# Ones woven between pairs of x tiles for a 65-column read matmul, and x transposed by DMA block by block

## The chip, the cores and the metric

The kernel runs on one core of a Trainium2 chip. The time is device microseconds (us) of that core. The kernel before takes 156.45 us, the median of three runs (155.93 to 156.77). The profile comes from one further execution, of 155.67 us, whose recorded span is 153.8 us.

## What is computed

A cross-attention between 512 tokens and 32 state rows for each of 8 batches and 8 heads, followed by a maxout feed-forward layer on the 8 x 544 = 4352 rows that it gives:

```python
scores = scale * x @ state.T                # per batch and head: 512 x 32
xread  = softmax(scores) @ state            # 512 x 64
sread  = softmax(scale * state @ x.T) @ x   # 32 x 64
rows   = concat([xread, sread], axis=2)     # heads side by side: 544 x 512 per batch
h      = max(rows @ w1, rows @ w2, rows @ w3)   # 512 -> 768
out    = h @ w_out                              # 768 -> 512
```

Both softmaxes use the same exponentials: `exp(scores)` is normalised along the states for `xread` and along the tokens for `sread`. So `sread` is a matmul of the exponentials with x, and its denominators are the same exponentials times a column of ones.

## The kernel before

All data is cast to bf16. The tokens of a batch lie as 128 partitions by 4 (`j`), so x of one batch is one tile of 128 x 2048, with 64 columns of ones behind it (width `XW + D`, lines 66 and 437). GpSimd issues the loads, one DMA of 512 KB (as written) per batch (`load_x`, line 70). For the products x must be transposed: for batches 0 to 2 TensorE does it (`x_transpose`, line 174, with a copy out of PSUM at line 178); for batches 3 to 7 one DMA transpose of the whole tile does it, 128 x 2048 into 16 blocks of 128 x 128, issued from the SyncE queue (`x_transpose_dma`, line 182). The rest of a batch goes as follows.

- `scores` (L196) multiplies the transposed x, 16 blocks as stationary operand, with the states, and ScalarE takes the exponential into `e` (L201).
- `softmax` (L208 to L211) gives the normalised `a`; its last multiplication runs on GpSimd. `a_transpose_dma` (L227) transposes `a` into `aT`, one DMA transpose of 8 blocks, for batches 3 to 7.
- The first layer's weights are folded with the states first: `G` = state x w1, w2, w3 (L271, L278 and L281), so `x_maxout` multiplies `aT` with `G` directly (L343), and ScalarE and VectorE take the maximum of three products (L347, L350, L351). `ffn_out` is the second layer (L381, copied out at L384, stored at L392 and L395).
- `sread` (L241) does 32 matmuls a batch, with 32 columns of `e` as stationary operand and 128 moving columns: 64 columns of x and the 64 ones. Four heads' results share a PSUM tile by rows, at column tiles of the array. VectorE takes the reciprocal of the denominators and multiplies (L246, L248), giving `sr`; a small DMA transpose of one 128 x 128 block puts it into `ats` (L249). Its issue is put off in the list `late`.
- The 256 rows of `sread` of all batches go through the feed-forward layer as a batch "s", interleaved with batch 7.

The schedule is manual: each engine runs its instructions in the order in which the program writes them, and so does the SyncE queue. From batch 2 on, a loop over `b` lays the work of batch `n = b + 1` into six slots between the six `x_maxout` blocks of batch `b`: `scores(n)` in slot 0, `softmax(n)` in slot 1, `a_transpose_dma(n)` and then `x_transpose_dma(n + 2)` in slot 2, `sread(n)` in slot 4, and the put-off `ats` transposes in slot 5. So `aT` of batch n is issued after x of batch n + 1 and before x of batch n + 2, and `x_maxout(n, 0)` needs that `aT`. The tile `xT` has three buffers. On the SyncE queue the order from the first DMA transpose on is: xT of batch 3; the states of two pairs of batches (`stT`, L143); `ats` of batches 0, 1 and 2; xT 4; aT 3; xT 5; ats 3; aT 4; xT 6; ats 4; aT 5; xT 7; ats 5; aT 6; ats 6; aT 7; ats 7; and then stores.

Of the kernel before, what the change touches and what calls it, by code (L numbers as in the profile page):

```python
# [8 lines left out]
F32 = mybir.dt.float32  # L9
BF16 = mybir.dt.bfloat16  # L10
AX = mybir.AxisListType
# [4 lines left out]
def kernel(  # L16
# [14 lines left out]
    nc = tc.nc  # L31

    B, H, S, D = x.shape
# [8 lines left out]
    J = 4  # L42
    HS = H // 2
    NM = d_ff // 128
    XW = H * J * D
# [3 lines left out]
    data = ctx.enter_context(tc.tile_pool(name="data", bufs=1))  # L49
    wpool = ctx.enter_context(tc.tile_pool(name="weights", bufs=1))  # L50
    work = ctx.enter_context(tc.tile_pool(name="work", bufs=2))
    pp = ctx.enter_context(tc.tile_pool(name="pp", bufs=2, space=bass.MemoryType.PSUM))
# [10 lines left out]
    load_st(0, nc.sync)  # L63


    x_sb = [data.tile([128, XW + D], BF16, name=f"x{b}") for b in range(B)]
    xv = [t[:, 0:XW].rearrange("p (h j d) -> p h j d", j=J, d=D) for t in x_sb]

    def load_x(b):
        nc.gpsimd.dma_start(  # L70
            out=x_sb[b][:, 0:XW].rearrange("p (h jd) -> p h jd", h=H),
            in_=x[b].rearrange("h (p j) d -> p h (j d)", j=J))

    def x_heads(b, g):
        return (x_sb[b][:, 0:XW].rearrange("p (s g jd) -> g p s jd", g=2, s=HS)[g],
# [10 lines left out]
    ident = const.tile([128, 128], BF16, name="ident")  # L86
# [73 lines left out]
    xT, e, a, aT, G, ht, osb = {}, {}, {}, {}, {}, {}, {}  # L160

    def new(d, b, shape, name, bufs=2):
        d[b] = work.tile(shape, BF16, tag=name, bufs=bufs, name=name)

    def x_transpose(b, g, *copies):

        if g == 0:
            new(xT, b, [128, H, 2, 128], "xT", bufs=3)
        n = HS // len(copies)
        for k, copy in enumerate(copies):  # L170
            p = pp.tile([128, n, 2, 128], BF16, tag="pw", bufs=4, name="pxt")
            for s in range(n):
                for jj in range(2):
                    nc.tensor.transpose(  # L174
                        p[:, s, jj, :],
                        xv[b][:, 2 * (n * k + s) + g, 2 * jj:2 * jj + 2, :].rearrange("p j d -> p (j d)"),
                        ident)
            copy(out=xT[b].rearrange("p (s g) j t -> p g s j t", g=2)[:, g, n * k:n * k + n], in_=p)  # L178

    def x_transpose_dma(b):  # L180
        new(xT, b, [128, H, 2, 128], "xT", bufs=3)
        nc.sync.dma_start_transpose(out=xT[b].rearrange("p h j t -> p (h j) t"), in_=x_sb[b][:, 0:XW])

    def scores(b, g0, g1):
        n = g1 - g0
# [45 lines left out]

    def sread(b):

        p = pp.tile([128, 2, 2, D], F32, tag="pw", bufs=4, name="psr")
        for j in range(J):
            for g in range(2):
                for s in range(HS):
                    xj = xv[b][:, 2 * s + g, j, :]
                    both = bass.AP(xj.tensor, xj.offset,
                                   (xj.ap[0], (XW - ((2 * s + g) * J + j) * D, 2), (1, D)))  # L240
                    nc.tensor.matmul(  # L241
                        p[32 * s:32 * s + 32, g], e[b][:, j, g, s, :], both,
                        start=(j == 0 and g == 0), stop=(j == J - 1), skip_group_check=True,
                        tile_position=(0, 32 * s))
        rd = work.tile([128, 2, 1], F32, tag="rd", name="rd")
        nc.vector.reciprocal(out=rd, in_=p[:, :, 1, 0:1])  # L246
        sr = work.tile([128, 2, D], BF16, tag="sr", bufs=B, name="sr")
        nc.vector.tensor_mul(out=sr, in0=p[:, :, 0, :], in1=rd.to_broadcast((128, 2, D)))  # L248
        late.append(lambda: nc.sync.dma_start_transpose(  # L249
            out=ats[:, b].rearrange("p s n -> p (s n)"), in_=sr.rearrange("p g d -> p (g d)")))  # L250

# [154 lines left out]
    for cast, r in ((dve, slice(0, 2)), (act, slice(2, 4))):  # L406
        cast(out=x_heads(0, 0)[0][:, r], in_=x0_f[:, r])
    x_transpose(0, 0, dve, act)
    x_transpose(0, 1, dve, dve)
    scores(0, 0, 1)  # L410
    softmax(0, 0, 1, nc.gpsimd.tensor_mul)
# [3 lines left out]
    softmax(0, 1, 2, nc.vector.tensor_mul)  # L415
    keep_busy(2)
    x_transpose(1, 0, act)
    keep_busy(6)
    scores(1, 0, 1)
# [8 lines left out]
    softmax(1, 1, 2, nc.gpsimd.tensor_mul)  # L428
    load_st(1, nc.gpsimd)
    load_x(2)  # L430
    nc.gpsimd.dma_start(out=wout_sb, in_=moe_w_out.rearrange("(kk p) f -> p kk f", p=128))
    for k in range(2, B // 2):
        load_st(k, nc.gpsimd)
    load_x(3)
    load_x(4)
    for b in range(2, B):
        nc.gpsimd.memset(x_sb[b][:, XW:XW + D], 1.0)
    for k in range(1, B // 2):
        nc.gpsimd.memset(bds[k], 0.0)
    g_cols(0, (1,))  # L440
    g_cols(1, (0,))
    sread(0)
    sread(1)
    x_maxout(0, 1)
    a_transpose(1, 0, act)
# [19 lines left out]
    scores(2, 0, 2)  # L465
    softmax(2, 0, 2, nc.gpsimd.tensor_mul)
    x_transpose_dma(3)
    for k in range(2, B // 2):
        states_transpose(k, True)
# [3 lines left out]
    ffn_out(0, 1)  # L473
    load_x(5)
    sread(2)
    g_front(2)
    for k in range(2, B // 2):
# [5 lines left out]
    ffn_out(0, 3)  # L483
    late_transposes()
    x_transpose_dma(4)


    for b in range(2, B):
        n = b + 1
        slots = [[] for _ in range(NM)]  # L490
        if n < B:
            slots[0].append(lambda: scores(n, 0, 2))
            slots[1].append(lambda: softmax(n, 0, 2, nc.gpsimd.tensor_mul))
            slots[2].append(lambda: a_transpose_dma(n))
            if n + 2 < B:
                slots[2].append(lambda: x_transpose_dma(n + 2))
            slots[5].append(late_transposes)
            if n + 3 < B:
                slots[0].append(lambda: load_x(n + 3))
        else:  # L500
            for m in range(NM):
                slots[m].append(lambda m=m: s_maxout(m))
        slots[1].append(lambda: g_back(b))
        if n < B:
            slots[4].append(lambda: sread(n))
            slots[4].append(lambda: g_front(n))
        for j, m in enumerate((1, 2, 4, 5)):
            slots[m].insert(0 if m > 2 else len(slots[m]), lambda j=j: ffn_out(b - 1, j))
        for m in range(NM):
            x_maxout(b, m)  # L510
            for f in slots[m]:
                f()
# [36 lines left out]
```

## Time and profile before

| engine | busy us | share of the 153.8 us span | instructions |
|---|---|---|---|
| TensorE, matmuls | 147.5 | 96% | 1389 |
| VectorE | 96.6 | 63% | 171 |
| ScalarE | 94.9 | 62% | 147 |
| GpSimd | 53.7 | 35% | 76 |

| group | instructions | from the page or the tile's view |
|---|---|---|
| L241 matmuls of `sread` | 256, 128 columns each | 4.9 us busy |
| L70 loads of x, batches 2 to 7 | 6 | 0.93 us of GpSimd each, landing after 6.2 to 13.8 us |
| L182 transpose of x by DMA | 5, 16 blocks each | 3.0 to 4.0 us of the queue each, landing after 4.6 to 8.7 us |
| L227 transpose of `a` by DMA | 5, 8 blocks each | 1.24 us of the queue each, landing after 3.7 to 4.8 us |
| L249 transpose of `sr` by DMA | 8, one block each | 1.12 to 1.43 us of the queue each, landing after 2.2 to 5.9 us |

Each engine's busy time is what its instructions last. The SyncE queue does no arithmetic and is not in the first table; its DMA instructions show in the timeline of that queue with a start and a duration, and the DMA views give the time from issue to landing.

### The profile page before, as it was taken

What the parts mean: (1) busy time and instruction counts of PE and PEld (TensorE: products, weight loads), DVE (VectorE), ACT (ScalarE), POOL (GpSimd) and SP (SyncE); (2) the same over time, 40 slices, a digit from 0 to 9 for tenths busy, and PEclk for the clock granted to TensorE, in tenths of its full rate; (3) what the DMA queues carried; (4) which work ended last, traced back from release to release, by engine and by line L of the source; (5) the groups of instructions that cost most, each with busy time, mean ns of one, the idle gap of its engine ahead of it and who ended that gap; (6) DMA issues with size and microseconds to landing.
All of it is one profiled execution on the core that took longest, in us unless ns stands there. A gap on an engine that the chain in (4) does not pass through costs nothing.

```text
span 153.8 us, 3487 instructions
## 1 busy us (share of the span) xinstructions
PE 147.5 (96%) x1389; PEld 72.0 (47%) x1389; DVE 96.6 (63%) x171; ACT 94.9 (62%) x147; POOL 53.7 (35%) x76
## 2 busy tenths in 40 slices
PE   6999899999999999999999999999999999999990
PEld 2556333454453445344534453445344556655450
DVE  3469867859727676767676767675767583565100
ACT  3686687885758656865686568646865637333340
POOL 8979899113990603060106010601060100100050
PEclk9999999999999999999999999999999999999998
DMA  4999999999698995959820972070306030110375
GB/s 123 193 183 192 193 218 203 235 196 156 79 188 228 236 290 115 178 89 258 98 108 11 231 136 112 27 184 21 124 19 190 18 131 0 61 78 0 141 232 177
DMA packets 36736, 21.72 MB, mean 141 GB/s; under 512 B 21968, under 2 KB 34384, under 8 KB 36720
## 3 DMA queue, kind: packets, MB, share of 16 engines
q0 software_dynamic: 17232, 15.08, 50.6%
q1 hardware_dynamic: 19344, 6.29, 21.9%
q8 instruction: 11, 0.18, 0.4%
q10 hardware_dynamic: 144, 0.13, 0.2%
q14 instruction: 5, 0.04, 0.1%
HBM read 15.20 MB, written 8.91 MB: 157 GB/s over the span
## 4 chain that ended last, share of the span: by engine, by line
PE 83%; DVE 5%; DMA 4%; POOL 3%; ACT 1%; issue 1%; DVEq 0%; POOLq 0%
PE pw L343 43%; PE po L381 28%; PE pg L271 4%; DMA x<-in_x_dram 4%; PE psr L241 2%; PE ps L196 2%; POOL w L109 1%; DVE ht L351 1%; DVE t L350 1%; PE pg L297 1%; POOL x L80 1%; PE pxt L174 1%; PE ph L373 1%; DVE den L208 1%; ACT t L347 1%
## 5 line engine op out<-in xcount | busy, mean ns | idle before, releaser
L343 PE MATMUL pw<-aT,G 128*128 128x512 bf16 x288 | 69.5, 379 | 0.7 <-DVE sr L248 0.3
L350 DVE TENSOR_TENSOR t<-t,pw 128x512 bf16<-128x512 bf16 (+1 forms) x54 | 35.0, 649 | 30.3 <-ACT t L347 29.2
L381 PE MATMUL po<-wout,ht 128*128 128x512 bf16 x198 | 47.4, 379 | 0.2 <-DVE t L350 0.2
L343 PEld LDWEIGHTS <-G 128*128 128x128 bf16 x288 | 26.9, 98 | 33.3 <-issue 4.0
L351 DVE TENSOR_TENSOR ht<-t,pw 128x512 bf16<-128x512 bf16 (+1 forms) x54 | 35.5, 658 | 6.0 <-DVE t L350 0.5
L384 ACT COPY osb<-po 128x512 f32<-128x512 f32 x33 | 19.3, 586 | 29.6 <-PE po L381 29.6
L347 ACT CAST t<-pw 128x512 bf16<-128x512 f32 (+1 forms) x54 | 30.5, 566 | 9.2 <-PE pw L343 8.3
L381 PEld LDWEIGHTS <-ht 128*128 128x128 bf16 x198 | 18.8, 98 | 23.9 <-issue 2.8
L395 POOL DMA_DIRECT2D out_dram<-osb x14 | 7.9, 562 | 55.1 <-ACT osb L384 45.8
L278 ACT CAST G<-pg 128x1024 bf16<-128x1024 f32 x24 | 24.5, 1021 | 3.6 <-PE pg L271 3.1
L211 POOL TENSOR_TENSOR a<-e,rden 128x1024 bf16<-128x1024 bf16 (+1 forms) x9 | 14.6, 1627 | 31.4 <-ACT t L347 15.4
L208 DVE TENSOR_REDUCE den<-e 128x32 f32<-128x1024 bf16 (+1 forms) x10 | 9.9, 995 | 0.8 <-ACT e L201 0.8
L303 ACT CAST G<-pg 128x768 bf16<-128x768 f32 x11 | 8.7, 809 | 2.0 <-PE pg L297 1.9
L109 POOL DMA_DIRECT2D w<-in_moe_w_dram x12 | 9.0, 780 | 0.0
L343 PE MATMUL pw<-ats,w 128*128 128x256 bf16 x72 | 8.8, 273 | 0.0
L201 ACT ACTIVATE e<-ps 128x1024 bf16<-128x1024 f32 x6 | 6.2, 1032 | 3.7 <-PE ps L196 3.7
L126 PE MATMUL idle<-zero 128*128 128x512 bf16 x19 | 7.0, 508 | 1.2 <-DVE zero L85 1.2
L343 PEld LDWEIGHTS <-w 128*128 128x128 bf16 x72 | 7.0, 98 | 2.1
L271 PE MATMUL pg<-w,bd 64*32 64x512 bf16 x192 | 7.5, 381 | 0.0
L196 PEld LDWEIGHTS <-xT 128*128 128x128 bf16 x128 | 4.9, 98 | 2.3 <-ACT xT L178 0.6
L70 POOL DMA_DIRECT2D x<-in_x_dram x6 | 5.5, 926 | 0.0
L281 DVE CAST G<-pgs 128x256 bf16<-128x256 f32 x12 | 4.5, 420 | 1.1 <-PE pgs L271 1.1
(55 smaller groups left out, 83.1 us busy)
## 6 DMA issues: line engine op xcount, KB each, us to landing
out_dram<-osb POOLq DMA_DIRECT2D x14, 512.0 KB, 3.5
x<-in_x_dram POOLq DMA_DIRECT2D x6, 512.0 KB, 8.7
w<-in_moe_w_dram POOLq DMA_DIRECT2D x6, 256.0 KB, 7.2
x<-in_x_dram POOLq DMA_DIRECT2D x3, 256.0 KB, 5.9
w<-in_moe_w_dram POOLq DMA_DIRECT2D x6, 128.0 KB, 6.0
wout<-in_moe_w_out_dram POOLq DMA_DIRECT2D x1, 768.0 KB, 10.6
x0f<-in_x_dram SPq DMA_DIRECT2D x1, 512.0 KB, 3.8
out_dram<-osb SPq DMA_DIRECT2D x1, 512.0 KB, 2.7
```

What stands on the lines that cost most here:

```text
L109: nc.gpsimd.dma_start(out=w_slices(w_sb, c)[:, :, i, :], in_=w[:, :, m0 * 128:m1 * 128])
L208: nc.vector.reduce_sum(out=den, in_=e[b][:, :, g0:g1], axis=AX.X)
L211: mul(out=a[b][:, :, g0:g1].rearrange("p j g s n -> p j (g s) n"), in0=e[b][:, :, g0:g1].rearrange("p j g s n -> p j (g s) n"), in1=rden.r ...
L271: nc.tensor.matmul(ps[g][32 * s:32 * s + 32], bd(b, 2 * s + g)[64 * g:64 * g + 64, g, :], w_sb[64 * g:64 * g + 64, s, c0:c1], start=True, ...
L278: copy(out=G[b][:, :, c0:c1], in_=p[:, :, 0:n])
L303: copy(out=m_cols(G[b], m), in_=pv)
L343: nc.tensor.matmul(p[:, 0:n], lhs(i, k), rhs(k), start=(k == 0), stop=(k == nk - 1))
L347: nc.scalar.copy(out=t0[:, 0:n], in_=pw[0][:, 0:n])
L350: nc.vector.tensor_max(t1[:, 0:n], t0[:, 0:n], pw[1][:, 0:n])
L351: nc.vector.tensor_max(ht[b][:, m, :], t1[:, 0:n], pw[2][:, 0:n])
L381: nc.tensor.matmul(p, ht[b][:, m, j * 128:(j + 1) * 128], wout_sb[:, m, :], start=(m == 0), stop=(m == NM - 1))
L384: act(out=o[:, j, :], in_=p)
```

## The change

For batches 2 to 7, x is stored in pairs: two 64-column tiles of x, then 16 columns of ones, so a pair takes `PW` = 144 columns, with 16 ones also ahead of the first. Each 64-column tile thus has a one right before it or right behind it, and `sread` moves a run of 65 columns in place of 64 columns of x and 64 ones. For even `j` the run starts with the one and for odd `j` it ends with it, so the two halves of a denominator gather in two PSUM columns, which a new `reduce_sum` on VectorE adds. The purpose is fewer moving columns on TensorE.

What comes with the layout: a `load_x` is two DMAs, one for each pair of `j`, each writing 128 x 8 runs of 128 elements where one DMA wrote 128 x 8 runs of 256, after a memset of the ones, 128 x 17 x 16; the six memsets of 128 x 64 at line 437 go. The transposes of x by DMA for batches 3 to 7 become 16 instructions of one 128 x 128 block each, as the source is no longer one unbroken row. Batches 0 and 1 keep their layout and their 128-column matmuls, and batch 2 is still transposed on TensorE.

```diff
-    x_sb = [data.tile([128, XW + D], BF16, name=f"x{b}") for b in range(B)]
-    xv = [t[:, 0:XW].rearrange("p (h j d) -> p h j d", j=J, d=D) for t in x_sb]
+    PAD = 16
+    PW = 2 * D + PAD
+    x_sb = [data.tile([128, XW + D if b < 2 else (2 * H + 1) * PW], BF16, name=f"x{b}") for b in range(B)]
+
+    def x_pairs(b):
+
+        if b < 2:
+            return x_sb[b][:, 0:XW].rearrange("p (h j d) -> p h j d", h=H, j=2)
+        return x_sb[b][:, PAD:PAD + 2 * H * PW].rearrange("p (h j d) -> p h j d", j=2, d=PW)[:, :, :, 0:2 * D]
 
     def load_x(b):
-        nc.gpsimd.dma_start(
-            out=x_sb[b][:, 0:XW].rearrange("p (h jd) -> p h jd", h=H),
-            in_=x[b].rearrange("h (p j) d -> p h (j d)", j=J))
+        nc.gpsimd.memset(x_sb[b].rearrange("p (k d) -> p k d", d=PW)[:, :, 0:PAD], 1.0)
+        for jj in range(2):
+            nc.gpsimd.dma_start(
+                out=x_pairs(b)[:, :, jj], in_=x[b].rearrange("h (p j t) d -> j p h (t d)", j=2, t=2)[jj])
...
     def x_transpose_dma(b):
         new(xT, b, [128, H, 2, 128], "xT", bufs=3)
-        nc.sync.dma_start_transpose(out=xT[b].rearrange("p h j t -> p (h j) t"), in_=x_sb[b][:, 0:XW])
+        for h in range(H):
+            for jj in range(2):
+                nc.sync.dma_start_transpose(out=xT[b][:, h, jj], in_=x_pairs(b)[:, h, jj])
...
     def sread(b):
 
-        p = pp.tile([128, 2, 2, D], F32, tag="pw", bufs=4, name="psr")
+
+        padded = b >= 2
+        p = pp.tile([128, 2, 2 * D], F32, tag="pw", bufs=4, name="psr")
         for j in range(J):
+            c0 = 1 if padded and j % 2 == 0 else 0
             for g in range(2):
                 for s in range(HS):
-                    xj = xv[b][:, 2 * s + g, j, :]
-                    both = bass.AP(xj.tensor, xj.offset,
-                                   (xj.ap[0], (XW - ((2 * s + g) * J + j) * D, 2), (1, D)))
+                    xj = x_pairs(b)[:, 2 * s + g, j // 2, D * (j % 2):D * (j % 2) + D]
+                    cols = ((1, D + 1),) if padded else ((XW - ((2 * s + g) * J + j) * D, 2), (1, D))
+                    both = bass.AP(xj.tensor, xj.offset - c0, (xj.ap[0], *cols))
+                    c = slice(1 - c0, D + 2 - c0) if padded else slice(0, 2 * D)
                     nc.tensor.matmul(
-                        p[32 * s:32 * s + 32, g], e[b][:, j, g, s, :], both,
+                        p[32 * s:32 * s + 32, g, c], e[b][:, j, g, s, :], both,
                         start=(j == 0 and g == 0), stop=(j == J - 1), skip_group_check=True,
                         tile_position=(0, 32 * s))
+        den = p[:, :, D:D + 1]
+        if padded:
+            den = work.tile([128, 2, 1], F32, tag="rs", name="rs")
+            nc.vector.reduce_sum(out=den, in_=p[:, :, 0:D + 2:D + 1], axis=AX.X)
         rd = work.tile([128, 2, 1], F32, tag="rd", name="rd")
-        nc.vector.reciprocal(out=rd, in_=p[:, :, 1, 0:1])
+        nc.vector.reciprocal(out=rd, in_=den)
...
-    for b in range(2, B):
-        nc.gpsimd.memset(x_sb[b][:, XW:XW + D], 1.0)
```

More of the change, by code (lines that the diff above doesn't have):

```diff
@@ L175, in x_transpose @@
                         p[:, s, jj, :],
-                        xv[b][:, 2 * (n * k + s) + g, 2 * jj:2 * jj + 2, :].rearrange("p j d -> p (j d)"),
-                        ident)
+                        x_pairs(b)[:, 2 * (n * k + s) + g, jj], ident)
             copy(out=xT[b].rearrange("p (s g) j t -> p g s j t", g=2)[:, g, n * k:n * k + n], in_=p)
@@ L232, in sread @@
     def sread(b):
-        p = pp.tile([128, 2, 2, D], F32, tag="pw", bufs=4, name="psr")
+        padded = b >= 2
+        p = pp.tile([128, 2, 2 * D], F32, tag="pw", bufs=4, name="psr")
         for j in range(J):
+            c0 = 1 if padded and j % 2 == 0 else 0
             for g in range(2):
                 for s in range(HS):
-                    xj = xv[b][:, 2 * s + g, j, :]
-                    both = bass.AP(xj.tensor, xj.offset,
-                                   (xj.ap[0], (XW - ((2 * s + g) * J + j) * D, 2), (1, D)))
+                    xj = x_pairs(b)[:, 2 * s + g, j // 2, D * (j % 2):D * (j % 2) + D]
+                    cols = ((1, D + 1),) if padded else ((XW - ((2 * s + g) * J + j) * D, 2), (1, D))
+                    both = bass.AP(xj.tensor, xj.offset - c0, (xj.ap[0], *cols))
+                    c = slice(1 - c0, D + 2 - c0) if padded else slice(0, 2 * D)
                     nc.tensor.matmul(
-                        p[32 * s:32 * s + 32, g], e[b][:, j, g, s, :], both,
+                        p[32 * s:32 * s + 32, g, c], e[b][:, j, g, s, :], both,
                         start=(j == 0 and g == 0), stop=(j == J - 1), skip_group_check=True,
                         tile_position=(0, 32 * s))
+        den = p[:, :, D:D + 1]
+        if padded:
+            den = work.tile([128, 2, 1], F32, tag="rs", name="rs")
+            nc.vector.reduce_sum(out=den, in_=p[:, :, 0:D + 2:D + 1], axis=AX.X)
         rd = work.tile([128, 2, 1], F32, tag="rd", name="rd")
-        nc.vector.reciprocal(out=rd, in_=p[:, :, 1, 0:1])
+        nc.vector.reciprocal(out=rd, in_=den)
         sr = work.tile([128, 2, D], BF16, tag="sr", bufs=B, name="sr")
-        nc.vector.tensor_mul(out=sr, in0=p[:, :, 0, :], in1=rd.to_broadcast((128, 2, D)))
+        c = slice(1, D + 1) if padded else slice(0, D)
+        nc.vector.tensor_mul(out=sr, in0=p[:, :, c], in1=rd.to_broadcast((128, 2, D)))
         late.append(lambda: nc.sync.dma_start_transpose(
```

## The prediction

> **What bounds the kernel now.** I read the page's first part, then the chain, then, because the change touches DMA transposes, the timeline of the SyncE queue and the waits of that queue. The page's busy times and the chain:
>
> ```profile
> PE 147.5 (96%) x1389; PEld 72.0 (47%) x1389; DVE 96.6 (63%) x171; ACT 94.9 (62%) x147; POOL 53.7 (35%) x76
> ...
> PE 83%; DVE 5%; DMA 4%; POOL 3%; ACT 1%; issue 1%; DVEq 0%; POOLq 0%
> ```
>
> TensorE (PE) is busy nearly throughout and is 83% of the chain. The chain in order of time (start us, us) shows one batch period:
>
> ```profile
> 45.09 0.47 PE ps L196 x16
> ...
> 55.28 0.56 PE psr L241 x32
> ...
> 59.20 1.29 PE pw L343 x6
> 60.50 0.47 PE ps L196 x16
> ```
>
> `scores(3)` starts at 45.09 and `scores(4)` at 60.50: a period is 15.4 us, solid TensorE work. A `sread` is 0.56 us of it. The first `x_maxout(3, 0)` is at 59.20; by the same view that of batch 6 starts at 105.51. The SyncE queue (start us, us, what):
>
> ```profile
> 32.94 3.26 SPq L182 DMA_TRANSPOSE xT<-x  x1
> 36.25 2.56 SPq L143 DMA_TRANSPOSE stT<-st  x2
> 38.85 3.78 SPq L249 DMA_TRANSPOSE ats<-sr  x3
> 42.79 3.02 SPq L182 DMA_TRANSPOSE xT<-x  x1
> 52.60 1.24 SPq L227 DMA_TRANSPOSE aT<-a  x1
> 54.01 3.81 SPq L182 DMA_TRANSPOSE xT<-x  x1
> 57.92 1.18 SPq L249 DMA_TRANSPOSE ats<-sr  x1
> 67.74 1.24 SPq L227 DMA_TRANSPOSE aT<-a  x1
> ```
>
> Two things are to be seen. First, what one instruction costs hardly depends on its blocks up to 8: one block (`ats`) 1.18 to 1.26, four (`stT`) 1.28, eight (`aT`) 1.24; sixteen (`xT`) 3.0 to 3.8. Second, the queue is busy 1.24 + 3.8 + 1.2 = 6.2 us of a 15.4 us period and otherwise waits. What it waits for (us in total, times, longest):
>
> ```profile
> SPq L227 <- POOL a L211: 42.6, 5, 9.8
> SPq L182 <- DMA x<-in_x_dram: 25.2, 1, 25.2
> ```
>
> Its slack is about 9 us a period, spent waiting for `a`; and its first transpose of x starts when x of batch 3 has landed, at 32.9.
>
> [...]
>
> **The change part by part.**
>
> *Read matmuls.* 192 of the 256 go from 128 to 65 columns. 32 of them take 0.56 us, 17.5 ns each[...]. If columns set it, 0.56 x 65/128 = 0.28 us, a gain of 0.28; if their weight loads do (0.46 us for 32 in the same stretch), 0.10. I take 0.2 us a batch: 6 x 0.2 = 1.2 us, bounds 0.6 and 1.7. This is all that the change can gain.
>
> *Denominator.* Six `reduce_sum` of 128 x 2 on VectorE; the trace has the reciprocal of that size at 0.17 us. VectorE is 63% busy and `sr` is wanted late, so 6 x 0.17 = 1.0 us is hidden; behind it on VectorE stand the two copies of G (L281), 0.4 us each, and at worst TensorE sees 0.1 us a batch.
>
> *Loads.* Six more DMA issues on GpSimd at 0.9 us each and memsets of 128 x 272, between the 0.22 us of 128 x 64 and the 1.02 us of 128 x 1024, say 0.35, in place of 0.22: 6 x (0.9 + 0.13) = 6.2 us on an engine with 100 us free. Until 26 us it is packed: behind it the cast of the states of batches 2 and 3 slips by about 3 us, which can hold TensorE at 28.5 for about 1 us; that is before the wait below, which absorbs it. The runs written are 256 B and not 512 B. The loads of the weights show both: 179 GB/s when nearly all packets are under 512 B (12 to 13 us), 195 GB/s when few are (14 to 15 us). So 512 KB take 0.25 us longer; x of batch 3, behind x of batch 2, lands about 0.5 us later, at 33.5.
>
> *Transposes by DMA.* This decides. Five instructions become 80. Three `ats` stand back to back at 38.85 and two `stT` at 36.25; their starts are 1.28 to 1.31 us apart. I take 1.28 us for each block: 16 x 1.28 = 20.5 us in place of 3.0 to 4.0. Bounds: 1.12 (shortest `ats`) and 1.43 (longest). The SyncE queue then needs 20.5 + 1.28 (`aT`) + 1.28 (`ats`) = 23.0 us per batch, against TensorE's 15.4. The slack of 9 us is less than the added 16.7. The queue becomes the bound, and it is in order: behind xT of batch n + 1 waits `aT` of batch n, and behind that `x_maxout(n, 0)` and all of TensorE.
>
> Worked along: xT 3 from 33.5 to 54.0, its last block landed at about 56 (`ats` lands 3.7 after issue at the median); `scores(3)` wanted it at 45.09, a stall of about 10.5. Then two `stT` and three `ats` (5 x 1.28) to 60.4, xT 4 to 80.9, and only then `aT` 3, landing 4.6 later at 85.5, where `x_maxout(3, 0)` was at 59.2: 26 us late. From there each batch comes 23.0 us after the last. The last `aT` behind an xT is that of batch 6 (there is no xT 8). Ahead of it from 33.5 are 80 xT, 2 `stT`, 6 `ats`, 3 `aT`, 91 instructions: 33.5 + 91 x 1.28 + 4.6 = 154.6, against 105.51 before: 49.1 us late. After that the queue is ahead again and TensorE does its last 48 us as before, with one waking of the clock: [...] I take 1.5. The gain of the reads counts only for batch 7, 0.2; the earlier ones end in the wait. Sum: 49.1 + 1.5 - 0.2 = 50.4; 156.45 + 50.4 = 206.9, say 207 us.
>
> **Rivals.** *A, the cost goes by blocks.* If a block in a row of such instructions costs 3.8/16 = 0.24 us, the queue's load is unchanged, nothing waits, and the reads' 1.2 us is left: 155.3 us, faster. For it: 16-block transposes cost more than 8-block ones. Against: three one-block instructions back to back took 1.28 us each. Chance 0.04. [...] Chance 0.04. *C, a dearer block.* [...] landings grew to 8.7 us beside loads; at 1.43 us a block, 33.5 + 91 x 1.43 + 4.6 = 168.2, 62.7 late: 220 us. [...] Chance 0.17. *The forecast,* 1.18 to 1.36 us a block, 198 to 214 us: chance 0.75.
>
> **How the numbers follow.** The time is that of the forecast. A tenth of a microsecond a block is 9 us at the end, so the shortest `ats`, 1.12, gives 33.5 + 91 x 1.12 + 4.6 - 105.5 = 34.5 late, 192 us, and C gives 220; I add the doubt on the clock and on landings and take 190 to 223. A and B are left out, and the far end of C. Faster is A, 0.04; within 0.5% is a part of B, 0.01; slower the rest, 0.95.
>
> **What would show it.** In the timeline of the SyncE queue, 80 transposes of one block about 1.28 us apart with no wait between from about 33.5 to 150; in the waits of TensorE, a stall of some 10 us before `scores(3)`, of some 15 us more before `x_maxout(3, 0)`, and of some 7.6 before those of batches 4 to 6, each on a DMA; TensorE's busy share near 72% (147 of 204 us of span), with clock digits below 9 after each stall; the matmuls of L241 shorter by about a third. If those blocks start less than 0.6 us apart, the prediction is wrong from its main step on; if they are 1.28 apart and the time is still near 156, something other than `aT` and xT sets TensorE's pace.

## The result and the profile after

The changed kernel takes 213.02 us (median of four runs, 212.49 to 214.11), the kernel before 156.61 us beside it: a ratio of 1.361, 95% interval 1.354 to 1.369. The forecast was 207 us, 190 to 223. In every ratio here, executions more than 1.5% above the fastest of their kernel are left out.

The page of the changed kernel, its busy times, its clock row and its chain (lines of the kernel have moved: L182 is now L192, L196 is L206, L227 is L237, L241 is L255, L249 is L268, L343 is L362):

```profile
PE 156.5 (74%) x1373; PEld 74.4 (35%) x1389; DVE 98.0 (46%) x177; ACT 95.4 (45%) x147; POOL 60.1 (28%) x82
...
PEclk9999999997589975599965899769995899999999
...
SPq 52%; PE 25%; DMA 11%; POOL 5%; issue 3%; DVE 1%; ACT 0%; POOLq 0%; DVEq 0%
SPq L192 49%; PE pw L362 14%; PE po L400 9%; DMA x<-in_x_dram 8%; SPq L237 2%; SPq L268 2%; DMA xT<-x 1%; DMA aT<-a 1%; POOL x L80 1%; PE pg L290 1%; POOL w L118 1%; POOL x L89 1%; POOL stf L58 1%; PE ph L392 1%; PE ps L206 1%
```

Before, TensorE was 83% of the chain and the SyncE queue (SPq) was not in it. Now that queue is 52%, and 49% is one line: the 80 transposes of single blocks. TensorE's own work has hardly grown (156.5 us against 147.5, part of it at a lower clock); its share fell because the span grew. The timeline of the SyncE queue (start us, us, what):

```profile
32.51 23.38 SPq L192 DMA_TRANSPOSE xT<-x  x16
55.99 2.52 SPq L152 DMA_TRANSPOSE stT<-st  x2
58.61 3.73 SPq L268 DMA_TRANSPOSE ats<-sr  x3
62.50 22.27 SPq L192 DMA_TRANSPOSE xT<-x  x16
84.89 1.26 SPq L237 DMA_TRANSPOSE aT<-a  x1
86.31 22.33 SPq L192 DMA_TRANSPOSE xT<-x  x16
...
159.27 1.25 SPq L237 DMA_TRANSPOSE aT<-a  x1
```

One xT took 3.0 to 4.0 us of this queue and now takes 21.4 to 23.4. From 32.5 to the `aT` of batch 6 at 159.3 the queue hardly rests: its longest gap is under half a microsecond. What TensorE waits for (us in total, times, longest):

```profile
PE pw L362 <- DMA aT<-a: 38.1, 4, 15.9
...
PE ps L206 <- DMA xT<-x: 9.2, 4, 4.6
```

Four waits for `aT`, the longest 15.9 us, and 9.2 us within `scores(3)`. Their sum, 47.3 us, is most of the 58.5 us by which the profiled span grew (212.3 - 153.8); TensorE's matmuls account for another 9.0, as the clock row falls as low as 5 in the slices of the waits and just after them.

### The profile page after: what moved, and what is told of

Same layout as the page of the kernel before. It is cut to its first block, busy times and chain, and to the rows that moved or that the text cites. A ratio compares the mean times of both kernels' runs of the same rounds, so it can differ in the third digit from the quotient of the medians.

```text
span 212.3 us, 3569 instructions
## 1 busy us (share of the span) xinstructions
PE 156.5 (74%) x1373; PEld 74.4 (35%) x1389; DVE 98.0 (46%) x177; ACT 95.4 (45%) x147; POOL 60.1 (28%) x82
## 4 chain that ended last, share of the span: by engine, by line
SPq 52%; PE 25%; DMA 11%; POOL 5%; issue 3%; DVE 1%; ACT 0%; POOLq 0%; DVEq 0%
SPq L192 49%; PE pw L362 14%; PE po L400 9%; DMA x<-in_x_dram 8%; SPq L237 2%; SPq L268 2%; DMA xT<-x 1%; DMA aT<-a 1%; POOL x L80 1%; PE pg L290 1%; POOL w L118 1%; POOL x L89 1%; POOL stf L58 1%; PE ph L392 1%; PE ps L206 1%
## 5 line engine op out<-in xcount | busy, mean ns | idle before, releaser
L362 PE MATMUL pw<-aT,G 128*128 128x512 bf16 x288 | 77.5, 411 | 38.6 <-DMA aT<-a 38.1
L362 PEld LDWEIGHTS <-G 128*128 128x128 bf16 x288 | 28.1, 103 | 76.4 <-issue 51.6
L366 ACT CAST t<-pw 128x512 bf16<-128x512 f32 (+1 forms) x54 | 30.5, 565 | 49.2 <-PE pw L362 48.3
L400 PE MATMUL po<-wout,ht 128*128 128x512 bf16 x183 | 46.6, 379 | 1.0 <-DVE t L369 0.2
L206 PE MATMUL ps<-bd,xT 128*128 128x64 bf16 x96 | 6.3, 227 | 9.2 <-DMA xT<-x 9.2
L206 PEld LDWEIGHTS <-xT 128*128 128x128 bf16 x128 | 7.0, 116 | 13.4 <-DMA xT<-x 9.8
L80 POOL DMA_DIRECT2D x<-in_x_dram x12 | 10.9, 927 | 0.0
L362 PE MATMUL pw<-ats,w 128*128 128x256 bf16 x72 | 8.8, 272 | 0.0
L161 POOL COPY bd<-stT 64x512 bf16<-64x512 bf16 x4 | 4.2, 1061 | 16.2 <-DMA stT<-st 16.1
L362 PEld LDWEIGHTS <-w 128*128 128x128 bf16 x72 | 7.1, 98 | 2.1
```

Of the source, the lines that this page charges most:

```text
L80: nc.gpsimd.dma_start(out=x_pairs(b)[:, :, jj], in_=x[b].rearrange("h (p j t) d -> j p h (t d)", j=2, t=2)[jj])
L206: nc.tensor.matmul(p[:, 2 * jj:2 * jj + 2, g - g0, s, :], xT[b][:, h, jj, :], bd(b, h).rearrange("p c n -> p (c n)"), start=(g == g0 and s ...
L362: nc.tensor.matmul(p[:, 0:n], lhs(i, k), rhs(k), start=(k == 0), stop=(k == nk - 1))
L366: nc.scalar.copy(out=t0[:, 0:n], in_=pw[0][:, 0:n])
L400: nc.tensor.matmul(p, ht[b][:, m, j * 128:(j + 1) * 128], wout_sb[:, m, :], start=(m == 0), stop=(m == NM - 1))
```

## The experiments

Two rivals to the queue's cost per instruction had to be told from it: L, that the padded layout or its loads are the cause, and D, that the DMA engines are slow over single blocks. Later came O, that only the order on the queue is at fault.

### The transposes alone: 16 blocks out of the plain layout

```diff
-        nc.sync.dma_start_transpose(out=xT[b].rearrange("p h j t -> p (h j) t"), in_=x_sb[b][:, 0:XW])
+        for h in range(H):
+            for jj in range(2):
+                nc.sync.dma_start_transpose(out=xT[b][:, h, jj], in_=xv[b][:, h, 2 * jj:2 * jj + 2, :].rearrange("p j d -> p (j d)"))
```

> The kernel before with one edit: its transpose of x by DMA is cut into 16 instructions of one 128 x 128 block. The layout of x, the loads and the 128-column reads stay. Theory (the SyncE queue's cost per instruction, 1.28 us and some 1.4 beside stores, times 80, is what the change costs): the whole loss comes back, 213 us, 209 to 217, as the reads give at most 0.2 us after the last stall. Rival L (the padded rows, their 288-byte steps and the loads in shorter runs make transposes and loads slow): near 156.6, at most 160. Rival D (the DMA engines take longer over single blocks, not the queue over issuing them): also slow, but then the transposes' durations on the queue stay short and their time from issue to landing grows beyond 5 us.

Measured: 212.66 us (212.14 to 213.56), ratio 1.359, 1.353 to 1.365. That is the whole loss, without any padding. The timeline of its SyncE queue:

```profile
33.59 21.69 SPq L184 DMA_TRANSPOSE xT<-x  x16
...
61.91 21.59 SPq L184 DMA_TRANSPOSE xT<-x  x16
83.60 1.25 SPq L229 DMA_TRANSPOSE aT<-a  x1
```

The plain rows give the same 21.6 us for 16 blocks, so L is out as the cause of the loss. For D the changed kernel's own answer serves, in the view of L192 (duration on the queue in ns, then from issue to landing in us):

```profile
L192 SPq DMA_TRANSPOSE xT<-x x80: 1093/1230/3387, 32.5 to 156.3; - x80
DMA to landing us min/median/max: 2.2/2.4/6.8
```

With the plain rows the median landing is 2.4 us too. At the median a block lands sooner than the `ats` of the kernel before (3.7), and it holds the queue for 1.23 us: D is out. In a kernel shown below, in which no load or store runs from 66 to 150 us, these transposes keep the DMA engines busy for only 16% of that time.

### Fewer cuts: 8 and 2 instructions

The edit for 8 instructions of two blocks is shown; the other kernel has 2 of eight blocks, cut in the same way.

```diff
-        nc.sync.dma_start_transpose(out=xT[b].rearrange("p h j t -> p (h j) t"), in_=x_sb[b][:, 0:XW])
+        for q in range(8):
+            nc.sync.dma_start_transpose(
+                out=xT[b].rearrange("p h j t -> p (h j) t")[:, 2 * q:2 * q + 2, :],
+                in_=x_sb[b][:, 256 * q:256 * q + 256])
```

> The kernel before with its transpose of x by DMA cut into 8 instructions of two blocks. Theory: 8 x 1.3 + 2.5 = 13 us of queue a batch fit into the period of 15.4, so there is no stall in every batch, only one at the start: xT of batch 4 ends near 61, aT of batch 3 lands near 64 where it was wanted at 59.2: 161 us, 158 to 164. Rival D, or any cost that goes with the blocks or with each split evenly: half of the loss of 16, near 184.

> The kernel before with its transpose of x by DMA cut into 2 instructions of eight blocks. Theory: 2 x 1.28 = 2.6 us in place of 3.0 to 4.0, all in the queue's slack: no change, 156.2 to 157.0, and each instruction of eight blocks at 1.25 us on the queue. Rival (every split costs its share of the loss, 56 us over 15 cuts a batch): 160.

Two instructions: 156.91 us beside 156.41, ratio 1.002 (1.000 to 1.005), no change, as the theory has it. Its xT take 2.6 to 4.0 us of the queue, no more than before; halved, an instruction of eight blocks took 1.3 to 2.0 us, where 1.25 was expected. Here the cut cost nothing, as the queue was busy for some 6 of the 15.4 us of a period.

Eight instructions: 172.73 us (170.14 to 174.19), ratio 1.094, 1.085 to 1.103. That is neither the 161 of the theory nor the 184 of an even cost. At the median an instruction of two blocks took 1.25 us, as one of a single block does (1.23) and one of eight (`aT`, 1.24): up to eight blocks, the price goes by the instruction. The waits of its profile show that the shape was right and the size wrong:

```profile
PE pw L346 <- DMA aT<-a: 11.9, 1, 11.9
```

There is a single wait for `aT`, as expected, and none in the later batches; but it is 11.9 us, where some 5 were worked out. Its chain (start us, us, what) says why:

```profile
54.12 3.00 SPq L183
...
57.17 1.72 SPq L183
...
58.93 1.67 SPq L183
...
66.59 8.87 DMA aT<-a
```

Instructions of two blocks took 1.6 to 3.0 us here, beside stores issued at 53 and a load of x at 54; `aT` was issued 1.4 us after another load of x, and landed 8.9 us later. I had taken 1.3 and some 3. That bulk transfers beside them are the reason is read from the times; no run of this kernel leaves them out.

### One batch alone: 16 blocks for batch 7 only

```diff
-        nc.sync.dma_start_transpose(out=xT[b].rearrange("p h j t -> p (h j) t"), in_=x_sb[b][:, 0:XW])
+        if b < B - 1:
+            nc.sync.dma_start_transpose(out=xT[b].rearrange("p h j t -> p (h j) t"), in_=x_sb[b][:, 0:XW])
+            return
...
```

> The kernel before with only batch 7's transpose of x by DMA cut into 16 instructions. Theory: xT of batch 7 starts at 84.5 as before and takes 16 x 1.4 = 22.4 us to 106.9; ats of batch 5 follows, then aT of batch 6 at 108.2, landing 3.1 later at 111.3 where it was wanted at 105.5: 5.8 us late, and up to 1.5 for the clock: 162 to 164 us, as 9 us of the 18.5 more on the queue lie in its slack. Rival (each split batch costs a fifth of the loss, whatever slack the queue has): 156.6 + 56/5 = 168.

Measured: 166.05 us (164.79 to 167.0), ratio 1.061, 1.053 to 1.069, or 164.7 to 167.2 us. The median lies 2 us above the theory's range and 2 below the rival's 168, so the time alone does not decide. The timeline and chain of the profiled run (164.79 us) do:

```profile
84.71 22.86 SPq L187 DMA_TRANSPOSE xT<-x  x16
107.67 1.51 SPq L254 DMA_TRANSPOSE ats<-sr  x1
109.29 1.25 SPq L232 DMA_TRANSPOSE aT<-a  x1
```

```profile
112.49 2.72 PE pw L348 x6
```

In the chain of the kernel before, the same matmuls of `x_maxout(6, 0)` stand at

```profile
105.51 1.29 PE pw L343 x6
```

The queue was 22.9 us over this xT, 19 more than before, and TensorE went on 7.0 us behind the kernel before. So the slack took up 12 of the 19 us, in the way that the theory says, with `aT` issued 1.1 us later than worked out.

### The order on the queue

In this version of the changed kernel, `aT` of batch n is issued between the two halves of xT of batch n + 1:

```diff
...
             slots[2].append(lambda: a_transpose_dma(n))
+            if n + 1 < B:
+                slots[2].append(lambda: x_transpose_dma(n + 1, 4, 8))
             if n + 2 < B:
-                slots[2].append(lambda: x_transpose_dma(n + 2))
+                slots[2].append(lambda: x_transpose_dma(n + 2, 0, 4))
```

> The changed kernel with another order on the SyncE queue: aT of batch n is issued after the first 8 blocks of xT of batch n + 1, not after all 16. Theory (the queue's load, some 24 us a batch against 15.4 of TensorE, is the bound, and order does not change it): as the changed kernel, 213 us, 205 to 218. Rival O (it is aT's place behind 16 blocks that costs; with half of them ahead half of the loss goes): 180 to 190.

Measured: 211.78 us (210.69 to 212.32), ratio 1.355, 1.349 to 1.361. O is out: with the first `aT` issued at 73.2 in place of 84.9 the end comes only 1.2 us sooner, since TensorE then waits for the later half of xT (9.2 us before this edit):

```profile
PE ps L207 <- DMA xT<-x: 29.7, 16, 4.0
```

While the queue is the bound, its load counts and this order does not.

### What makes a block dearer than 1.28 us

In the changed kernel 91 instructions lie between 32.51 and 159.27, 1.39 us each. Two runs take bulk transfers away. The first leaves out the stores of batches 1 to 6, the second also the loads of x for batches 5 to 7.

```diff
-        elif b < B - 1 and j >= 2:
+        elif b == 0 and j >= 2:
```

```diff
+    for b in range(5, B):
+        x_sb[b] = x_sb[4]
...
     def load_x(b):
+        if b > 4:
+            return
...
```

> The changed kernel without the stores of the results of batches 1 to 6 (12 of the 14 stores of L414 are left out; these rows are not written). In the changed kernel a block took 1.28 us in quiet stretches and up to 3.4 us in single cases, 1.39 us on average from the first xT to aT of batch 6; most of the long ones follow a store or a load of x by a microsecond or two. Theory (bulk transfers hold up the issue of transposes): about half of the 10 us of excess goes, 207 to 210 us. Rival (the average block is just dearer than the three in a row of before, whatever else runs): 213.

> As the one without stores, and also without the loads of x for batches 5 to 7, which use the tile of batch 4 (the results of these batches are those of another x). No bulk transfer then runs beside the transposes from about 40 us on. Theory: nearly all blocks at 1.28 us: 32.5 + 91 x 1.28 + 3.2 = 152.2, 46.7 late, 1.5 for the clock: 204.6 us, 203 to 207. Rival: 213.

Measured: 211.29 us (210.02 to 211.35) without stores and 208.94 us without both. Both are above what was expected, if below 213. By the issue of `aT` of batch 6, at 155.34 and 153.47 us, the mean is (155.34 - 32.31)/91 = 1.352 and (153.47 - 32.13)/91 = 1.333 us. So bulk transfers are 0.06 of the 0.11 us above 1.28, and not nearly all. The chain of the quiet kernel shows some of the rest:

```profile
99.13 1.24 SPq L197
100.41 1.78 SPq L197
102.24 1.23 SPq L197
```

Blocks start 1.27 us apart, and then one takes 1.78 with no load or store beside it; there is one like it in most xT (1.80 at 69.15, 1.63 at 122.97, 1.86 at 145.13). Within a microsecond of each of these four moves a packet of q8, one of two queues that the page lists as of the kind "instruction", as the DMA view of that kernel has it for 100 to 103 us:

```profile
q8 instruction: 1, 0.02, 2.1%
```

The kernel has only 11 packets of q8 in all. In this kernel, the changed one, the one without stores, the one with `aT` between the halves and the one of 16 plain blocks, each of the 25 packets of q8 between 50 and 155 us falls within a microsecond of a transpose of 1.56 to 2.54 us. This is hardly chance, but it was seen and not tried: whether these packets hold the queue up is open.

### Keeping the shorter reads

The reads gain, and the split transposes lose; can they be parted? First by loading batches 3 to 7 twice, plain for one DMA transpose and padded for the reads, and as a control the same loads with the reads of 128 columns from the plain copy:

```diff
...
+    x_plain = {b: data.tile([128, XW], BF16, name=f"xq{b}") for b in range(3, B)}
...
+    def load_pad(b):
         for jj in range(2):
             nc.gpsimd.dma_start(
                 out=x_pairs(b)[:, :, jj], in_=x[b].rearrange("h (p j t) d -> j p h (t d)", j=2, t=2)[jj])
...
+        nc.sync.dma_start_transpose(out=xT[b].rearrange("p h j t -> p (h j) t"), in_=x_plain[b])
...
```

> A version meant to keep the gain and leave out the loss: batches 3 to 7 are loaded twice, once plain for one DMA transpose of 16 blocks as before, once padded for the reads of 65 columns (two more DMAs of 256 KB a batch on GpSimd, issued after the softmax). Batch 2 stays as before. Theory: the reads of five batches are 0.2 us shorter each, 1.0 us in all, and the second loads lie in time that the DMA engines have: 155.4 us, 154.9 to 156.2. Rival L (the padded layout or the extra loads cost time themselves): 157 to 160.

> The same double loads, but the reads move 128 columns of the plain copy as before; the padded copy is loaded and not used. Theory: as the kernel before, 156.2 to 157.0, so that the difference to the version with two copies and 65 columns is the reads' 1.0 us. Rival L: 157 to 160 here too, from the loads.

Measured: 163.81 us at the median, scattered from 156.06 to 166.77, too wide for a ratio, and 164.45 us (161.41 to 165.47) for the control, ratio 1.036, 1.029 to 1.044, beside 156.27. Both medians miss what was expected: with the extra loads eleven of the twelve executions lose 3 to 11 us, with either kind of read, and one loses nothing. L was wrong for the layout and right for more loads. In the control's waits (profiled at 163.84 us) TensorE stands once for `aT`:

```profile
PE pw L371 <- DMA aT<-a: 4.2, 1, 4.2
```

and the times from issue to landing (min, median, max) of its transposes, first of `a`, then of x, from the views of the tiles aT and xT, are

```profile
DMA to landing us min/median/max: 4.5/5.9/9.2
```

```profile
DMA to landing us min/median/max: 8.2/16.1/20.5
```

Before they were 3.7/4.6/4.8 and 4.6/7.1/8.7. The `aT` that took 9.2 us is that of batch 3. By the control's chain its delay begins with `stT`, which landed 9.0 us after its issue (2.5 before): GpSimd's copies of it and the multiplication that makes `a` came later, and `aT` was issued at 54.10 (52.60 before), beside loads and a store. It landed 4.2 us after TensorE wanted it, and TensorE lost another 2.9 us, with the clock row at 6 and 5 in the two slices from 60.8 to 68.9 us and at 9 in all others: by its timeline the two `x_maxout` that come in a row in that batch start at 73.76, where the kernel before has them at 66.64. The transposes of x land in time all the same. The version with two copies was profiled at 156.06 us: its transposes of x land as late (15.6 us at the median), but its `stT` lands in 5.1 us, its `aT` of batch 3 is issued at 52.31, and TensorE does not wait for it. So the second loads have no fixed price; in these two profiles the loss goes with how late a few transposes land. Why that differs from run to run stays open.

So the padded copy was made on chip, by GpSimd, with no DMA more (the edit is against the version with two copies; the first copy also comes later in the program):

```diff
     def load_pad(b):
-        for jj in range(2):
-            nc.gpsimd.dma_start(
-                out=x_pairs(b)[:, :, jj], in_=x[b].rearrange("h (p j t) d -> j p h (t d)", j=2, t=2)[jj])
+        pool(out=x_pairs(b), in_=x_plain[b].rearrange("p (h j d) -> p h j d", h=H, j=2))
...
```

> The padded copy of x for batches 3 to 7 is made by GpSimd out of the plain tile (one copy of 128 x 2048 a batch, about 3 us, from the 1.9 us of its 128 x 1024 multiplication and the 0.64 us of its 128 x 512 cast) instead of by a second load; the transpose is one DMA of 16 blocks as before, and the reads of these five batches move 65 columns. GpSimd has about 10 us free in a period of 15.4. Theory (the read gains 0.2 us a batch once no DMA is added): 155.3, 154.8 to 155.9, against 156.3. Rival: GpSimd's copy holds up VectorE's work or the softmax on GpSimd, 156.3 or more.

Measured: 155.37 us (median of eleven runs) beside 156.47, ratio 0.993, interval 0.990 to 0.995: 1.1 us faster than the kernel before, as expected, and the fastest of all. That the gain is the reads' follows from its size (five reads of 0.2 us); no run has this copy with reads of 128 columns. The profile is of an execution of 160.51 us, so only durations are read from it. From its groups (busy us, mean ns) and its chain, where a `sread` is 0.36 us and was 0.56:

```profile
L86 POOL COPY x<-xq 128x2048 bf16<-128x2048 bf16 x5 | 9.4, 1887 | 0.1
L258 PE MATMUL psr<-x,e 128*32 128x65 bf16 (+1 forms) x256 | 3.9, 205 | 0.0
L265 DVE TENSOR_REDUCE rs<-psr 128x2 f32<-128x4 f32 x5 | 0.8, 162 | 1.5 <-PE psr L258 1.5
```

```profile
76.33 0.36 PE psr L258 x32
```

## Why the prediction was right

- *The queue becomes the bound.* Right: 80 transposes, hardly a rest from 32.5 to 159.3 us, and the loss came back whole with these transposes alone. Rival A (0.24 us a block) falls with the 1.23 us that a block takes at the median, and so does B, an estimate that had no figure of this case under it: no single block of the changed kernel took less than 1.09 us.
- *1.28 us a block* was the term of the sum that was too small. It measured 1.39 over the 91 instructions: 126.8 us in place of 116.5, 10.3 more. That is above the forecast's band of 1.18 to 1.36 and below C's 1.43. Most blocks are indeed 1.27 apart; the excess is in a few long ones, which the price from three `ats` of 1.23 us each could not show. Of the 80 blocks 14 took 1.4 us or more, up to 3.39, together 9.8 us above 1.23.
- *Start and landing* were taken too long, which by luck gave 2.5 us of it back: xT of batch 3 began at 32.5, not 33.5, and `aT` of batch 6 landed 3.1 us after issue, not 4.6. Without that the time would have left the band's 198 to 214, though not the whole range. By the chain TensorE went on at 162.48, where the forecast had 154.6:

```profile
162.48 2.72 PE pw L362 x6
```

- *The stalls*: 10.5 us before `scores(3)`, forecast, were 9.2; 15 more before `x_maxout(3, 0)` were 15.9; 7.6 in each of the next three were (38.1 - 15.9)/3 = 7.4. This last agreement is luck. From `x_maxout(3, 0)` to `x_maxout(6, 0)`, the changed kernel first and the kernel before below it (us, then TensorE's busy time; the clock is the third number from the end):

```profile
88.10:162.48 74.38, 51.89 (x439) 22.57 (x446) 32.76 (x57) 31.01 (x45) 9.15 (x9) 0.84 0.29 77
59.20:105.51 46.31, 46.31 (x446) 21.07 (x444) 32.15 (x55) 30.72 (x45) 10.02 (x10) 1.00 0.57 123
```

  A batch took 74.38/3 = 24.8 us, not 23.0, and TensorE's own work in it 51.89/3 = 17.3, not 15.4, as the clock granted was 0.84. The forecast had neither, and the two errors cancel in the stalls. The slower work between stalls costs nothing at the end, since the queue sets the pace there.

- *The clock*: 1.5 us. From 162.48 to the end at 212.3 are 49.8 us where the kernel before needs 48.3 from 105.5; with the 0.2 that the last read gains added, the clock is 1.7. The clock row falls to 5 about the stalls. In the last of them TensorE has nothing to do from 155.1 us; the clock granted is 1.00 until 159.0, 0.50 from 159.25 to 166.0, which is 3.5 us after TensorE went on, and 1.00 from 166.25. The trace before has no such wait and could not show it: the forecast's 1.5 was an estimate without a figure of that trace behind it.
- *The reads*: 0.2 us a batch was taken, between 0.10 and 0.28. A `sread` went from 0.56 to 0.36 us, and the version with GpSimd's copy ends 1.1 us sooner, about what five of them give.
- *The denominator and the loads on GpSimd.* The reductions took 0.16 us each, 0.17 was taken. The waits show a hold of TensorE of 0.78 us at 30 us, for the states' cast on GpSimd, as the forecast's "about 1 us"; it lies ahead of the wait for xT and cost nothing. The halved runs of the loads, priced at 0.5 us for x of batch 3, did not show: xT 3 started 0.4 us earlier than before, and in all four profiles of padded loads it started at 32.1 to 32.5, against 32.9 to 34.1 in the five of the kernel before and its cuts.

## What to carry to other kernels

Before cutting one DMA transpose into many, multiply the duration of a small one on the issuing queue by their number and compare it with the period of the engine that sets the end: here 2 instructions (2.6 to 4.0 us of 15.4), far below it, changed nothing, and 16 (21.4 to 23.4 us), beyond it, set the pace in both orders that were run (213.02 and 211.78 us). Close to that edge, leave room: 8 fitted by the sum, 13 us of 15.4, and still cost 16 us, as an instruction took up to 3.0 us, not 1.3, and `aT` landed after 8.9 us, not some 3. And where a layout serves one consumer and harms another, a copy on an engine with time to spare can be cheaper than either a second load or a worse transpose: here 1.9 us of GpSimd a batch gave 155.37 us, the second load 156.06 to 166.77, the split transpose 213.02.

## What was not expected of the hardware

- A second load of each x, 512 KB a batch, moved the median time from issue to landing of a 16-block transpose from 7.1 to 16.1 us in the control and 15.6 in the other version, and its duration on the queue up to 9.7 us in the control's timeline.
- In a stretch without loads or stores (66 to 150 us of the quiet kernel), 4 of 60 single-block transposes still took 1.6 to 1.9 us in place of 1.23, each time beside a packet of the "instruction" queue q8.
- A DMA transpose of one, two or eight blocks held the queue for about the same time: 1.23, 1.25 and 1.24 us in the three kernels that show them (the first two at the median).
- GpSimd copied 128 x 2048 bf16 in 1.89 us, as long as its multiplication of 128 x 1024 took before (1.91).
